# Attention, a mixture of four experts and a gated layer on one core: weight preparation issued earlier and in other steps

## Chip, core and metric

One core of one Trainium2 chip. The time is that of one execution on the device, in microseconds (us); the kernel before takes 738.04 us (median of three executions, 737.47 to 739.43). The engines run their own queues in order and meet at semaphores: TensorE (PE, with its weight loads as PEld), VectorE (DVE), ScalarE (ACT), GpSimd (POOL) and the queue that issues DMAs (SP).

## What is computed

Three layers in float32 precision, one feeding the next. `B, H, S, D = 2, 8, 576, 64`; 1152 tokens, model width 512.

```python
# 1. attention: heads 0..3 see the last 32 positions, heads 4..7 every 32nd one
scores = where(mask, q @ k.T / sqrt(64), -1e9)
attn = exp(scores - max); attn /= sum + 1e-9
x = (attn @ v) -> [1152, 512]
# 2. four experts, all applied to every token, mixed by normalised weights
p = domain_probs / (sum + 1e-9)
x = sum over e of p[:, e] * (relu(x @ w1[e]) @ w2[e])       # w1 512x1024, w2 1024x512
# 3. a gated layer; its three weights arrive as float64
out = (sigmoid(x @ w_gate) * (x @ w_val)) @ w_out            # 512x1536, 512x1536, 1536x512
```

## The kernel before

Every matrix product of layers 2 and 3 is done in halves: a float32 operand becomes a float16 part and a float16 remainder, and three products (high by high, high by low, low by high) are summed in PSUM (`split_products`, L552). Each operand is first scaled by a power of two found from its largest magnitude, on the chip.

**Units.** Layers 2 and 3 are 56 units. A unit is `("u", s, T)` (the first product of stage s on the T-th 288 tokens) or `("d", s, T)` (the second product). Stages 0 to 3 are the experts, 4 to 6 the three column blocks of the gated layer. A "u" unit of an expert has 8 PSUM tiles of 12 matmuls, a "d" unit of an expert 4 tiles of 24, so each has 96 matmuls of 288 columns. The order is u(0,0), d(0,0), u(0,1), d(0,1), ... for the first expert, and from then on u(1,0), u(1,1), d(1,0), u(1,2), d(1,1), ..., always with one "u" unit between a "u" and its "d".

**Attention** is a generator of 32 steps i = 0 to 31 (`attention`, L501). Step i normalises group i-1, multiplies group i-4 by the values, transposes the probabilities of group i-3, prepares queries and keys, and computes the scores of group i (24 groups). DVE takes the maximum, subtracts it and sums; ACT takes the exponential and copies PSUM tiles out. Steps 0 to 17 run in a loop of their own (`while 0 not in x_done`), because the first unit needs the scaled output of the first batch; steps 18 to 27 are issued inside u(0,0), one after every third group of three matmuls (`ATT_EVERY`); steps 28 to 31 stand between u(0,0) and d(0,0). `x_pair` scales a batch's result: it begins at step 15 for batch 0 and at step 27 for batch 1, with a maximum on DVE (L480, L485), a transpose on PE (L244) and a broadcast on PE (L250).

**Weights** come as 17 pieces (w1, w2 of each expert: pieces 0 to 7; gate, value and output block of each of three column blocks: 8 to 16). A piece is two raw tiles of 1 MB, which take turns in three buffers (`RAW_BUFS`). `prep_weights` is a generator, and each of its yields is one step:

- expert pieces: four maxima on DVE (L306), named R0 to R3 below; a last maximum over the four (L308), a transpose on PE (L244, "Ha") and a broadcast on PE (L250, "Hb"), after each of which the call ends ("hold"); then, once the weight buffer has room, four parts P0 to P3, each of them a scaled float16 copy on ACT (L332) and its remainder on DVE (L333, which reads what L332 wrote). Then it asks for two further raw tiles: their DMAs wait for the buffers that P1 and P3 release.
- float64 pieces: each half of a raw tile is turned into float32 by integer operations on DVE (`float32_of`, L263 to L279: L269, L271, L273, L275, L277, five steps), twice per raw tile; two maxima; Ha and Hb; then two parts with two ACT operations (L336, L337) and a remainder on POOL (L339).

Who calls it sets the order: `prep_some(n, steps)` goes on by so many steps. In the loop it is called with one step from i = 8 on, until piece 0 is done; in u(0,0) with one step after each of its 8 tiles; after the attention has ended, with two steps at each tile's "evac", which is before the instructions that empty that tile. Before a unit starts, what its own pieces still lack is prepared at once (L886).

**Emptying a tile.** In "u" units of experts ACT writes the float16 part and a copy (L595, L596), POOL the remainder (L597). In "d" units DVE scales the tile by the token weight into `t` (L616) and adds it to the sum over experts `x2acc` (L618); for the last expert it also takes the maximum (L620). After the last "d" tile of a T, `scale_x2` takes the maximum of four (L628), and `finish_x2`, a second generator that moves on once per tile (`go_late`), issues the transpose (L244), the broadcast (L250) and the scaled halves of the new x. Its first step is empty, so the transpose is issued one tile after L628.

The PE queue runs in order: a transpose Ha that waits for a DVE maximum holds all matmuls issued after it.

Of the kernel before, what the change touches and what calls it, by code (L numbers as in the profile page):

```python
# [9 lines left out]
F32 = mybir.dt.float32  # L10
# [8 lines left out]
PSUM = bass.MemoryType.PSUM  # L19

MASKED = -1.0e9
TOP = 2.0 ** 14
DOWN = 2.0 ** -24
W_BUFS = 2
# [12 lines left out]
def attn_moe_glu_kernel(ctx, tc, q, k, v, dp, w1, w2, wg, wv, wo, out):  # L37
# [48 lines left out]
    def load_local_qk(b, c):  # L86

        for nm, src in (("ql", q), ("kl", k)):
            t = atp.tile([TL, 2, 6 * D], F32, tag="raw" + nm, name="raw" + nm, bufs=1)
            nc.sync.dma_start(t, src[b, 2 * c:2 * c + 2].rearrange("h (p i) d -> p h (i d)", i=6))  # L90
            qkv["raw" + nm, b, c] = t
# [171 lines left out]
    def float32_of(f, r):  # L263

        words = r.bitcast(U32).rearrange("p (n z) -> p n z", z=2)
        lo_, hi_ = words[:, :, 0], words[:, :, 1]
        a = tmp["p"].tile([128, 512], U32, tag="bits", name="bits", bufs=1)
        m = tmp["p"].tile([128, 512], U32, tag="magn", name="magn", bufs=1)
        nc.vector.tensor_scalar(a, hi_, 5, 2, ALU.logical_shift_left, ALU.logical_shift_right)  # L269
        yield  # L270
        nc.vector.tensor_scalar(m, hi_, 1, None, ALU.logical_shift_left)  # L271
        yield
        nc.vector.scalar_tensor_tensor(a, hi_, 0xC0000000, a, ALU.bitwise_and, ALU.bitwise_or)  # L273
        yield
        nc.vector.scalar_tensor_tensor(a, lo_, 29, a, ALU.logical_shift_right, ALU.bitwise_or)  # L275
        yield
        nc.vector.scalar_tensor_tensor(  # L277
            f, m, float(897 << 21), a.bitcast(F32), ALU.is_ge, ALU.mult)
        yield  # L279

    peak_n = [0]
# [318 lines left out]
    def g2(e, T):  # L600
        pc = 2 * e + 1
        hh, hl = H.pop((e, T))
        col = e * NT + T
        cc = comb[:, col:col + 1]
        nc.vector.tensor_scalar(cc, down[:, 2 * e:2 * e + 1], down[:, SX + T:SX + T + 1], 1.0 / DOWN, ALU.mult, ALU.mult)
        nc.vector.tensor_tensor(cc, cc, down[:, pc:pc + 1], ALU.mult)
        for kk in range(KC):
            ps = g_tile()[:, :TC]
            yield from split_products(ps, [
                (wh[pc][:, fb, kk * 128:(kk + 1) * 128], wl[pc][:, fb, kk * 128:(kk + 1) * 128],  # L610
                 hh[fb], hl[fb]) for fb in range(FB)
            ])
            yield "evac"
            a = acc["x2"][:, kk, T * TC:(T + 1) * TC]
            t = a if e == 0 else scratch()
            nc.vector.scalar_tensor_tensor(t, ps, cc, pb[e, T], ALU.mult, ALU.mult)  # L616
            if e:
                nc.vector.tensor_tensor(a, a, t, ALU.add)  # L618
            if e == E - 1:
                nc.vector.tensor_reduce(  # L620
                    peak[:, 8 + kk:9 + kk], a, AX.X, ALU.max, apply_absolute_value=True)
            yield "tile"
        if e == E - 1:
            yield from scale_x2(T)
# [8 lines left out]

    def finish_x2(T, scale):

        yield
        yield from scale
        yield
        col = SX2 + T
        alloc_x(T)  # L640
        for kk in range(KC):
            a = acc["x2"][:, kk, T * TC:(T + 1) * TC]
            dh, dl = xh[T][:, kk, :], xl[T][:, kk, :]
            nc.scalar.activation(dh, a, AF.Copy, scale=up[:, col:col + 1])
            nc.vector.scalar_tensor_tensor(dl, a, up[:, col:col + 1], dh, ALU.mult, ALU.subtract)
        for r in range(T * TC // 128, -(-(T + 1) * TC // 128)):
            n = min((T + 1) * TC - r * 128, 128)
            if n == 128 and r * 128 >= T * TC:
                nc.vector.tensor_scalar(row_down[:, r:r + 1], down[:, col:col + 1], 1.0 / DOWN, None, ALU.mult)
            elif n < 128:  # L650
                nc.vector.tensor_scalar(row_down[:n, r:r + 1], down[:n, col:col + 1], 1.0 / DOWN, None, ALU.mult)
            else:
                p0 = T * TC - r * 128
                for q0, q1 in ((32, 64), (64, 96), (96, 128)):
                    if q0 >= p0:
                        nc.vector.tensor_scalar(
                            row_down[q0:q1, r:r + 1], down[q0:q1, col:col + 1], 1.0 / DOWN, None, ALU.mult)
        yield
# [154 lines left out]
    with tc.manual_schedule():  # L813
        load_strided_qk(0, 0)
        load_strided_qk(0, 1)
        load_strided_v(0, 0)
        load_local_qk(0, 0)
        load_strided_v(0, 1)
        load_local_v(0, 0)
        warm_up()  # L820
        make_constants()
        nc.scalar.activation(top[:, 0:1], ones[:, 0:1], AF.Exp)
        for T in range(NT):
            alloc_x(T)

        def more_loads():

            yield load_raw_to(1)
            yield load_local_qk(0, 1)
            yield load_local_v(0, 1)  # L830
            yield load_raw_to(2)
            yield load_strided_qk(1, 0)
            yield load_strided_v(1, 0)
            yield load_strided_qk(1, 1)
            yield nc.sync.dma_start(ptok, dp.rearrange("(t p) e -> p t e", p=128))
            yield load_local_qk(1, 0)
            yield load_strided_v(1, 1)
            yield load_local_v(1, 0)
            yield load_local_qk(1, 1)
            yield load_local_v(1, 1)  # L840
            yield load_raw_to(RAW_BUFS)


        load_at = {0: 1, 2: 1, 3: 2, 4: 1, 5: 1, 6: 1, 7: 1, 8: 1, 10: 1, 12: 1, 14: 1, 15: 1, 16: 1}
        mix_at = {1: (0, 0), 5: (0, 1), 13: (1, 0), 17: (1, 1)}
        loads = more_loads()

        def attend():
            i = next(att, None)
            if i is None:  # L850
                return None
            for _ in range(load_at.get(i, 0)):
                next(loads, None)
            if i in mix_at:
                mix_heads(*mix_at[i])
            if i == 12:
                token_weights()
            if i == 14:
                spread_token_weights()
            return i  # L860

        def end_attention():
            at_stack.close()
            accp = ctx.enter_context(tc.tile_pool(name="accp", bufs=1, side="right", reuse_waits="tile"))
            tmp["acc"] = accp
            tmp["p"] = ctx.enter_context(tc.tile_pool(name="tmp", bufs=2, side="right", reuse_waits="tile"))
            tmp["h"] = ctx.enter_context(tc.tile_pool(name="hp2", bufs=1, side="right", reuse_waits="tile"))
            tmp["g"] = ctx.enter_context(
                tc.tile_pool(name="gp2", bufs=8 - PSUM_BUFS, space=PSUM, side="right", reuse_waits="tile"))
            tmp["w"] = ctx.enter_context(tc.tile_pool(name="wp2", bufs=W_BUFS_2, side="right", reuse_waits="tile"))  # L870
            acc["x2"] = accp.tile([128, KC, NTOK], F32, tag="acc", name="x2acc")

        att = attention()
        while 0 not in x_done:
            i = attend()
            keep_warm(WARM_STEP)

            if i >= 8 and (going or todo[0] == 0):
                prep_some(0, 1)
        n_none = 0  # L880
        for n, u in enumerate(units):
            if n == 1:
                while "p" not in tmp:
                    if attend() is None:
                        end_attention()
            while any(i in pieces_of(u) for i in waiting()):  # L886
                prep_some(n, 1)
            if u[0] == "u" and u[1] >= E:
                go_late(u[2])
            if u == ("d", E, 0):  # L890
                go_late(NT - 1)
                acc["out"] = tmp["acc"].tile([128, NTB, DM], F32, tag="acc", name="outacc")
            load_p_some(n)
            load_p_some(n)
            for y in unit_steps(u):
                if "p" not in tmp and y is None:
                    n_none += 1
                    if n_none % ATT_EVERY == 0 and attend() is None:
                        end_attention()
                if y == ("tile" if "p" not in tmp else "evac"):  # L900
                    prep_some(n, 2 if "p" in tmp else 1)
                if y == "tile":
                    go_late()

# [27 lines left out]
```

## Time and profile before

The profiled execution took 736.88 us, of which 735.0 us lie between its first and last instruction; the median of the runs is 738.04 us.

| engine | busy us | share of the span | instructions |
|---|---|---|---|
| PE | 689.6 | 94% | 5702 |
| DVE | 419.9 | 57% | 812 |
| ACT | 265.8 | 36% | 568 |
| POOL | 210.0 | 29% | 257 |

The first unit's first matmul starts at 74.3 us, the unit d(0,0) at 115.3, u(0,1) at 136.5, u(4,0) at 501.8; the last instruction ends at 735.0. Unit borders are found by counting the matmuls of `split_products` in the order of time: 96 for each unit of an expert.

"Busy" is the time covered by instructions; a duration is that of one instruction; the idle time in brackets in a timeline is what the engine stood still before that instruction, and after the arrow is what ended it. The granted TensorE clock has two levels here, 1.2 and 2.4 GHz, and a stretch's mean of 0.70 means that it ran at half speed for 60% of it.

### The profile page before, as it was taken

Reading aid. Unit: us, or ns where it says so; the run is one execution under the profiler, and the core shown is the slowest. Engines: PE = TensorE matmul, PEld = TensorE weight load, DVE = VectorE, ACT = ScalarE, POOL = GpSimd, SP = SyncE. Lnnn points to the kernel's source line nnn. Section 1 sums busy time; section 2 is a strip of 40 time slices with the busy share of each in tenths; the row PEclk is TensorE's granted clock in tenths of the full one; section 3 lists DMA queues with packets and bytes.
Section 4 is the critical chain, followed back from the end, with each engine's and each line's share of the span. In section 5 each row is a group of like instructions: output and inputs, shape, how many; then the busy total and the mean of one; then the engine's idle time right before and its main releaser. Section 6 shows DMA issues by size and latency. Waiting matters only on the chain.

```text
span 735.0 us, 13594 instructions
## 1 busy us (share of the span) xinstructions
PE 689.6 (94%) x5702; PEld 512.6 (70%) x5713; DVE 419.9 (57%) x812; ACT 265.8 (36%) x568; POOL 210.0 (29%) x257
## 2 busy tenths in 40 slices
PE   8888695989998999999999999988899999999998
PEld 5656473767776777777777777767676666676774
DVE  2585867671066212639317797878887696822122
ACT  3544554433245125232324244252235344231220
POOL 4221230313214123114324272440224244141110
PEclk8997996989999999999999999999999999999999
DMA  8914302330033000304200221111111310000001
GB/s 220 229 30 123 131 2 91 138 133 9 9 123 115 7 4 10 123 9 172 66 9 26 99 66 58 58 58 58 58 58 58 115 58 1 1 1 1 29 29 72
DMA packets 26765, 48.88 MB, mean 67 GB/s; under 512 B 9324, under 2 KB 13200, under 8 KB 26704
## 3 DMA queue, kind: packets, MB, share of 16 engines
q1 hardware_dynamic: 26704, 48.02, 20.7%
q8 instruction: 45, 0.74, 0.4%
q14 instruction: 16, 0.13, 0.1%
HBM read 45.63 MB, written 2.38 MB: 65 GB/s over the span
## 4 chain that ended last, share of the span: by engine, by line
PE 74%; DVE 15%; ACT 5%; issue 2%; DMA 2%; POOL 1%; SPq 0%; ACTq 0%; DVEq 0%
PE gps L556 22%; PE gps L558 22%; PE gps L557 22%; DVE pk L306 3%; PE sps L412 2%; DVE wl L333 2%; ACT wh L332 1%; DVE cv L277 1%; DVE x2acc L618 1%; DVE t L616 1%; DMA ks<-in_k_dram 1%; DMA raw<-in_moe_w_dram 1%; DVE bits L275 1%; PE o L464 1%; DVE bits L273 1%
## 5 line engine op out<-in xcount | busy, mean ns | idle before, releaser
L557 PE MATMUL gps<-xl,wh 128*128 128x288 f16 x896 | 257.8, 288 | 1.1 <-DVE xl L495 1.1
L556 PE MATMUL gps<-xh,wh 128*128 128x288 f16 x896 | 258.0, 288 | 0.3 <-ACT xh L494 0.3
L558 PE MATMUL gps<-xh,wl 128*128 128x288 f16 x896 | 257.7, 288 | 0.0
L597 POOL TENSOR_TENSOR hl<-t,hh 128x288 f16<-128x288 f32 x128 | 104.8, 825 | 259.6 <-ACT t L596 256.3
L556 PEld LDWEIGHTS <-wh 128*128 128x128 f16 x1408 | 138.5, 98 | 41.4 <-ACT wh L332 4.5
L558 PEld LDWEIGHTS <-wl 128*128 128x128 f16 x1408 | 138.7, 99 | 39.5 <-DVE wl L333 2.3
L557 PEld LDWEIGHTS <-wh 128*128 128x128 f16 x1408 | 138.7, 98 | 36.2 <-issue 0.6
L556 PE MATMUL gps<-hh,wh 128*128 128x288 f16 x512 | 148.0, 289 | 3.7 <-ACT wh L332 3.7
L558 PE MATMUL gps<-hh,wl 128*128 128x288 f16 x512 | 147.9, 289 | 1.3 <-DVE wl L333 0.7
L557 PE MATMUL gps<-hl,wh 128*128 128x288 f16 x512 | 148.0, 289 | 0.0
L595 ACT ACTIVATE hh<-gps 128x288 f16<-128x288 f32 x128 | 52.4, 410 | 197.3 <-PE gps L558 197.3
L694 POOL TENSOR_TENSOR hl<-t,hh 128x288 f16<-128x288 f32 x48 | 37.5, 782 | 145.4 <-ACT hh L693 145.4
L616 DVE SCALAR_TENSOR_TENSOR t<-gps,comb,pb 128x288 f32<-128x288 f32 x48 | 24.6, 513 | 83.5 <-PE gps L558 82.1
L333 DVE SCALAR_TENSOR_TENSOR wl<-raw,up,wh 128x1024 f16<-128x1024 f32 x32 | 40.4, 1299 | 39.4 <-ACT wh L332 39.4
L596 ACT ACTIVATE t<-gps 128x288 f32<-128x288 f32 x128 | 51.9, 406 | 9.2 <-POOL hl L597 9.0
L692 DVE SCALAR_TENSOR_TENSOR t<-gps,sg 128x288 f32<-128x288 f32 x48 | 21.8, 454 | 54.0 <-PE gps L558 41.7
L339 POOL TENSOR_TENSOR wl<-cv,wh 128x1024 f16<-128x1024 f32 x18 | 40.3, 2239 | 40.5 <-ACT wh L337 40.5
L693 ACT CAST hh<-t 128x288 f16<-128x288 f32 x48 | 20.7, 431 | 80.8 <-DVE t L692 80.8
L332 ACT ACTIVATE wh<-raw,up 128x1024 f16<-128x1024 f32 x32 | 34.9, 1141 | 24.3 <-DVE up L236 13.4
L556 PE MATMUL gps<-wh,hh 128*128 128x512 f16 (+1 forms) x112 | 41.6, 371 | 0.0
L557 PE MATMUL gps<-wl,hh 128*128 128x512 f16 (+1 forms) x112 | 41.6, 371 | 0.0
L558 PE MATMUL gps<-wh,hl 128*128 128x512 f16 (+1 forms) x112 | 41.6, 371 | 0.0
(121 smaller groups left out, 727.0 us busy)
## 6 DMA issues: line engine op xcount, KB each, us to landing
raw<-in_moe_w_dram SPq DMA_DIRECT2D x16, 1024.0 KB
raw<-in_moe_w_gate_dram SPq DMA_DIRECT2D x6, 1024.0 KB
raw<-in_moe_w_val_dram SPq DMA_DIRECT2D x6, 1024.0 KB
raw<-in_moe_w_out_dram SPq DMA_DIRECT2D x6, 1024.0 KB
pb<-pd SPq DMA_DIRECT2D x15, 144.0 KB
out_dram<-outacc SPq DMA_DIRECT2D x8, 256.0 KB
vl<-in_v_dram SPq DMA_DIRECT2D x8, 192.0 KB
qs<-in_q_dram SPq DMA_DIRECT2D x4, 288.0 KB
```

The source lines that it names most:

```text
L306: nc.vector.tensor_reduce(pk[:, n:n + 1], part, AX.XY, ALU.max, apply_absolute_value=True)
L332: nc.scalar.activation(hi_, part, AF.Copy, scale=up[:, i:i + 1])
L333: nc.vector.scalar_tensor_tensor(lo_, part, up[:, i:i + 1], hi_, ALU.mult, ALU.subtract)
L339: nc.gpsimd.tensor_tensor(lo_, part, hi_, ALU.subtract)
L556: nc.tensor.matmul(ps, ah, bh, start=i == 0, stop=False)
L557: nc.tensor.matmul(ps, ah, bl, start=False, stop=False)
L558: nc.tensor.matmul(ps, al, bh, start=False, stop=i == n - 1)
L595: nc.scalar.activation(hh[fb], ps, AF.Relu, scale=DOWN)
L596: nc.scalar.activation(t, ps, AF.Relu, scale=DOWN)
L597: nc.gpsimd.tensor_tensor(hl[fb], t, hh[fb], ALU.subtract)
L616: nc.vector.scalar_tensor_tensor(t, ps, cc, pb[e, T], ALU.mult, ALU.mult)
L694: nc.gpsimd.tensor_tensor(dl, gv, dh, ALU.subtract)
```

## The change

In words: (1) in the attention loop `prep_some` is called from i = 6, with two steps at i = 6 and 7, and goes on to piece 1 from i = 16; inside u(0,0) it is also called with one step after every attention step, and with two steps instead of one after every tile. (2) The second raw tile is asked for before the values of heads 2 and 3, the third at i = 6 instead of i = 16, which puts it in front of four loads of batch 1. (3) In `float32_of` the magnitude is taken by ACT (`Abs`) in the first step, so there are four steps instead of five; the threshold is compared as a float. (4) The addition to `x2acc` goes from DVE to POOL. (5) `finish_x2` has one more empty step in front.

```diff
+LEAST = 2.0 ** -15 * 1.125
...
-        m = tmp["p"].tile([128, 512], U32, tag="magn", name="magn", bufs=1)
+        m = tmp["p"].tile([128, 512], F32, tag="magn", name="magn", bufs=1)
         nc.vector.tensor_scalar(a, hi_, 5, 2, ALU.logical_shift_left, ALU.logical_shift_right)
-        yield
-        nc.vector.tensor_scalar(m, hi_, 1, None, ALU.logical_shift_left)
+
+        nc.scalar.activation(m, hi_.bitcast(F32), AF.Abs)
         yield
...
         nc.vector.scalar_tensor_tensor(
-            f, m, float(897 << 21), a.bitcast(F32), ALU.is_ge, ALU.mult)
+            f, m, LEAST, a.bitcast(F32), ALU.is_ge, ALU.mult)
...
             if e:
-                nc.vector.tensor_tensor(a, a, t, ALU.add)
+                nc.gpsimd.tensor_tensor(a, a, t, ALU.add)
...
     def finish_x2(T, scale):
 
+        yield
         yield
         yield from scale
...
             yield load_raw_to(1)
             yield load_local_qk(0, 1)
+            yield load_raw_to(2)
             yield load_local_v(0, 1)
-            yield load_raw_to(2)
             yield load_strided_qk(1, 0)
             yield load_strided_v(1, 0)
+            yield load_raw_to(RAW_BUFS)
             yield load_strided_qk(1, 1)
...
-            yield load_raw_to(RAW_BUFS)
...
-        load_at = {0: 1, 2: 1, 3: 2, 4: 1, 5: 1, 6: 1, 7: 1, 8: 1, 10: 1, 12: 1, 14: 1, 15: 1, 16: 1}
+        load_at = {0: 1, 2: 2, 3: 1, 4: 1, 5: 1, 6: 1, 7: 1, 8: 2, 10: 1, 12: 1, 14: 1, 15: 1}
...
-            if i >= 8 and (going or todo[0] == 0):
-                prep_some(0, 1)
+            if 6 <= i and (going or todo[0] == 0 or i >= 16):
+                prep_some(0, 2 if i == 6 or i == 7 else 1)
...
-                    if n_none % ATT_EVERY == 0 and attend() is None:
-                        end_attention()
+                    if n_none % ATT_EVERY == 0:
+                        if attend() is None:
+                            end_attention()
+                        else:
+                            prep_some(n, 1)
                 if y == ("tile" if "p" not in tmp else "evac"):
-                    prep_some(n, 2 if "p" in tmp else 1)
+                    prep_some(n)
```

## Rows read from the trace of the kernel before

**Rows 1.** The page: busy us and share; the granted clock in 40 slices.

```profile
PE 689.6 (94%) x5702; PEld 512.6 (70%) x5713; DVE 419.9 (57%) x812; ACT 265.8 (36%) x568; POOL 210.0 (29%) x257
...
PEclk8997996989999999999999999999999999999999
```

**Rows 2.** The waits of PE: us in total, times, longest.

```profile
PE gps L244 <- DVE pk L308: 10.7, 5, 4.2
...
PE gps L244 <- DVE peak L628: 6.3, 4, 2.1
PE peaks L244 <- DVE peak L485: 4.0, 2, 2.8
PE gps L556 <- ACT wh L332: 3.7, 1, 3.7
```

**Rows 3.** Stretches: length, busy of PE, PEld, DVE, ACT, POOL, clock, DMA, GB/s.

```profile
45.90:60.25 14.35, 12.50 (x179) 8.97 (x179) 11.91 (x37) 7.19 (x21) 5.05 (x11) 1.00 0.16 45
...
92.07:103.60 11.53, 11.53 (x156) 8.33 (x153) 9.65 (x25) 5.81 (x18) 4.82 (x7) 1.00 0.01 3
...
115.30:136.50 21.20, 16.22 (x101) 10.56 (x100) 14.21 (x26) 6.90 (x12) 0.73 (x1) 0.70 0.33 114
136.50:155.70 19.20, 14.98 (x100) 10.79 (x100) 12.02 (x17) 10.68 (x20) 6.51 (x7) 0.82 0.30 110
...
203.30:215.00 11.70, 11.70 (x98) 9.36 (x96) 9.74 (x11) 4.86 (x6) 0.96 (x2) 1.00 0.51 179
215.00:227.30 12.30, 12.30 (x101) 9.70 (x100) 7.62 (x12) 8.48 (x17) 4.91 (x5) 1.00 0.23 65
227.30:242.60 15.30, 12.51 (x102) 9.65 (x100) 5.93 (x11) 6.08 (x17) 7.26 (x11) 1.00 0.27 97
301.40:314.40 13.00, 12.38 (x100) 9.59 (x99) 5.07 (x12) 5.09 (x14) 4.85 (x7) 1.00 0.06 21
...
471.20:487.90 16.70, 13.16 (x104) 9.83 (x103) 14.29 (x34) 6.75 (x19) 5.33 (x7) 1.00 0.34 123
487.90:501.80 13.90, 12.03 (x99) 9.42 (x99) 10.42 (x21) 4.74 (x6) 5.18 (x3) 1.00 0.00 1
```

**Rows 4.** Timelines of ACT and PE around attention step 18.

```profile
78.14 2.17 ACT L332 ACTIVATE wh<-raw,up 128x1024 f16<-128x1024 f32 x2
...
82.95 0.27 PE L377 MATMUL qkps<-ident,ql 96*128 96x96 f32 x1 [4.01 <-ACT PT L443]
```

**Rows 5.** Timeline of PE between the first two units.

```profile
113.56 0.27 PE L244 MATMUL peaks<-ident,peak 128*1 128x128 f32 x1 [2.78 <-DVE peak L485]
...
122.83 0.42 PE L556 MATMUL gps<-hh,wh 128*128 128x288 f16 x1 [3.71 <-ACT wh L332]
```

**Rows 6.** The chain that ended last, 136 to 160 us.

```profile
140.68 6.41 DMA raw<-in_moe_w_dram
```

**Rows 7.** Groups by line and form: busy us, mean ns, idle before.

```profile
L333 DVE SCALAR_TENSOR_TENSOR wl<-raw,up,wh 128x1024 f16<-128x1024 f32 x32 | 40.4, 1299 | 39.4 <-ACT wh L332 39.4
...
L306 DVE TENSOR_REDUCE pk<-raw 128x1 f32<-128x1024 f32 x32 | 37.7, 1208 | 1.3 <-DMA raw<-in_moe_w_dram 1.3
L332 ACT ACTIVATE wh<-raw,up 128x1024 f16<-128x1024 f32 x32 | 34.9, 1141 | 24.3 <-DVE up L236 13.4 <-PE gps L557 10.9
...
L618 DVE TENSOR_TENSOR x2acc<-x2acc,t 128x288 f32<-128x288 f32 x48 | 25.7, 535 | 1.6
...
L271 DVE TENSOR_SCALAR magn<-raw 128x512 uint32<-128x512 uint32 x36 | 19.4, 539 | 0.0
...
L428 POOL TENSOR_TENSOR P<-P,sm 128x288 f32<-128x288 f32 x24 | 16.0, 667 | 63.9 <-DVE sm L427 49.6 <-ACT ksT L384 4.7 <-PE o L474 3.1
```

**Rows 8.** Timelines of POOL and DVE in d(3,2).

```profile
490.65 4.45 POOL L339 TENSOR_TENSOR wl<-cv,wh 128x1024 f16<-128x1024 f32 x2 [1.48 <-ACT wh L337]
...
491.61 1.49 DVE L618 TENSOR_TENSOR x2acc<-x2acc,t 128x288 f32<-128x288 f32 x1
...
501.36 0.16 DVE L628 TENSOR_REDUCE peak<-peak 128x1 f32<-128x4 f32 x1
```

## The prediction

> **What bounds the kernel now.** First the page's busy times: PE is busy for 689.6 of 735.0 us [rows 1], so at most 45 us are idle, and every gain must come from PE's idle time or from its slow clock. Next the waits of PE [rows 2]: no engine's throughput stops it, but single late results do. Two kinds concern a transpose Ha that waits for a maximum of DVE: a weight piece's (10.7 us in 5) and the x2 scale's (6.3 in 4). Attention has 4.0 for batch maxima, d(0,0) 3.7 for a weight part. Then the table of stretches [rows 3] shows where: a unit of 96 matmuls at full clock takes 11.7 us (203.30:215.00, PE busy throughout), 0.12 each, so an expert "u" tile is 1.47 us and a "d" tile 2.94. Against that d(0,0) takes 21.2 at a mean clock of 0.70, u(0,1) 19.2 at 0.82, u(1,1) 15.3, u(3,3) 16.7, d(3,2) 13.9. The clock costs (1 - 0.70) x 21.2 = 6.4 and (1 - 0.82) x 19.2 = 3.5 us there, part of it on top of the idle time. Last the timelines: they name the late result at each place [rows 4, 5, 6].
>
> The sum is made against the profiled execution, 736.88 us; the median of the runs is 738.04, 1.16 above it. I add that back at the end.
>
> **Where each step lands.** Counting the calls by the code: before, R0 to R3 of piece 0 stand at i = 8 to 11 and P0 to P3 at i = 15, 16, 17 and in front of u(0,0); piece 1 gets one step per tile of u(0,0), so that its P2 and P3 come after the attention. After: R0 to R3 at i = 6, 7, the holds at 8 to 10, P0 to P3 at 11 to 14, R0 to R2 of piece 1 at 15 to 17. In u(0,0) there are 10 + 8 x 2 steps for 8: R3 at i = 18, Ha and Hb by the second tile, P0 at i = 20, P1 at i = 21, P2 and P3 behind the third tile, R0 of piece 2 at i = 22, R1 and R2 behind the fourth tile, R3 at i = 23. After its Ha and Hb, by i = 25, piece 2 only waits for room, which it has from d(0,0) on.
>
> **Part 1, the attention loop.** A part costs DVE 1.30 us and a wait for ACT's 1.14 us half; that wait averages 39.4 / 32 = 1.23 us [rows 7]. DVE's own attention work is about 1.95 us per step: 9.65 busy in four steps (92.07:103.60) less one and a half maxima of 1.21 [rows 3, 7]. With a part a step takes DVE 1.95 + 1.30 + 1.23 = 4.5 us; PE takes 14.35 / 4 = 3.6 per step at i = 11 to 14 [rows 3]. DVE falls behind by 0.9 x 4 = 3.6 us; what shows is between 0 (three score tiles lie ahead) and 3.6, as PE waits at i = 15 for a batch maximum behind all this; I take +2.5. Two maxima a step at i = 6 and 7 make DVE 1.95 + 2.42 = 4.4 us against 3.6: +0.5, between 0 and 1.6. The three maxima at 15 to 17 hide behind PE. Against that, two ACT halves leave step 18 [rows 4]: PE waits 4.01 us there behind 2.17 us of them, so -2.2; and P1's half no longer precedes the first x at i = 17, -1.1 (bounds 0 and its 1.14). The sum is -0.3, from -3.3 to +3.
>
> The third raw tile, 1 MB, goes before four batch 1 loads on SP. A lone raw tile takes 6.4 us [rows 6], the DMA queues are nearly empty from 45 to 60 us (share 0.16 [rows 3]), and these loads are used from step 12 on. I cost it at 0; if the cover fails, 6.4 at most.
>
> **Part 2, u(0,0) and d(0,0).** At i = 20 to 23 DVE gets 4 x 1.95 + 4 x 1.30 + three waits of 1.23 + 4 x 1.21 = 21.5 us in a stretch where PE needs 11.5 and idles nowhere [rows 3, 7]. It falls behind by 10 us. Two steps of 2.9 us fit in the score tiles; so +4, between 0 and 10. Steps 24 to 27 have no weight work, and DVE catches up there. So the maximum for x_pair at i = 27 no longer stands behind P0's remainder (1.30 us [rows 7]): of PE's 2.78 us wait for it [rows 5] I take half off, -1.4, between 0 and all of it. From that transpose to the end of d(0,0) it is 136.5 - 113.56 = 22.9 us now; work is left there for 6 + 96 matmuls x 0.1225 and a broadcast, 12.8. Piece 1 is ready, so the 3.71 us wait for a weight part [rows 5] goes, and with the idle time, I take it, the slow clock. Half a us is kept for the last remainder of POOL: -9.6, between -5 (slow clock stays) and -10. Part 2: 4.0 - 1.4 - 9.6 = -7.0.
>
> **Part 3, pieces 3 and 4.** Ha of a piece comes a fixed number of tiles behind P0 of the one before it, and between them lie P0, P1, a 6.41 us raw DMA that waits for P1's buffer, and two maxima [rows 6]. Piece 3 has five "u" tiles, 7.35 us, for this now and PE idles 4.2 us (longest in [rows 2]). After, P0 stands behind the first tile of d(0,0) and Ha behind the second of u(0,1): 3 x 2.94 + 2 x 1.47 = 11.8 us, as for piece 5, whose Ha in 215.00:227.30 costs nothing (12.30 busy of 12.30) [rows 3]. So u(0,1) falls from 19.2 to 12.3, like that unit: -6.9. Piece 4 then has 4 x 1.47 + 2.94 = 8.8 us. Piece 6, with 7.35, idles 2.8 (227.30:242.60) [rows 3]; less the 1.47 more that gives 1.3, and against piece 3's 4.2 it gives 2.7. I take +1.5. Part 3: -5.4, from -7 to -3.5. From unit 7 on the steps of expert pieces fall where they did.
>
> **Part 4, fourth expert on.** Idle now: of the 10.7 us of piece maxima [rows 2], 4.2 lie in u(0,1), 2.8 in u(1,1) and 0.6 in u(2,0) [rows 3], so 3.1 are left; with 6.3 for the four scales, 9.4 us. What changes:
> - `Abs` takes away 36 DVE instructions of 0.54 us [rows 7], 19 us in all, and 36 steps. A unit still makes two steps per tile, so a conversion ends earlier, but DVE's load per tile does not fall. On ACT it has no row; the 1024 column L332 takes 1.14 [rows 7], so at most that and above 0; half, 0.6, is taken. ACT is idle for over half of u(3,3) (6.75 busy of 16.70 [rows 3]), which hides it: 0; uncovered, 36 x 0.6 = 21 us of ACT.
> - The addition frees 0.535 us on DVE 48 times; for the second and third expert nothing waited for it, so 0. For the fourth, the maximum L620 behind it must now wait for POOL, and the next tile's steps behind L620. POOL's two-input L428 takes 0.67 [rows 7]; L339, 2.23 for 1024 columns [rows 8], gives 0.63 for 288. With both hand-overs I take 0.9, between 0.63 and the 1.49 of an addition that was slow on DVE [rows 8]. So each tile is 0.4 later and the maximum of a T 1.5: just the 1.47 that the x2 transpose now waits longer. Where POOL has two L339 in the same unit (d(3,2), 490.65 to 495.10 [rows 8]) the additions stand behind them, and I take 2.0.
> - Earlier conversions move the maxima: piece 10's out of u(3,2) into d(3,0), piece 11's into d(3,1), so DVE has less in front of the first two scales. Scales: d(3,2)'s 1.9 (13.90 less 12.03 [rows 3]) becomes 1.9 + 2.0 - 1.5 = 2.4; d(3,3)'s, the longest, goes from 2.1 to 1.6, as its L339 come late in the unit; the first two, 2.3 together, to 0.5. So 6.3 becomes 4.5. Pieces: 3.1 becomes 2.0, of which 1.2 is new (piece 12's Ha, now behind the first tile of d(3,3)). Together -2.9, between -8 and +3.
>
> The Trainium skill, "GPSIMD Engine Reference", section "Engine selection", puts GpSimd at about twice VectorE's time for elementwise operations of two inputs. By it an addition would take 1.07, some 0.4 more than L428 shows, the three scale waits that are left would grow by 1.6 each, and the sum would come out 4.8 later, a weaker form of rival 1. The trace does not bear it out: 0.67 against 0.535.
>
> **Sum.** -0.3 - 7.0 - 5.4 - 2.9 = -15.6: 736.88 - 15.6 = 721.3, and with 1.16 added 722.4 us.
>
> **Rivals.**
> 1. *POOL becomes DVE's brake.* In the fourth expert's "d" units DVE stops for POOL in all 16 tiles; if additions cost 1.49 each, a T's maximum is 4 x 0.95 = 3.8 us later, 2.3 more than the delay buys: four scales + 9.3, less some 6 that the moved maxima free in front of the first two, less 1.1 for the pieces. Part 4 is then +2.2, the time 727.5. For: [rows 8] show the addition on DVE at 1.49 against its mean of 0.535 while POOL runs. Against: POOL has 29% load [rows 1]. Chance 0.20.
> 2. *The new DVE load in attention takes the gain back.* One mechanism: DVE stands behind ACT's weight halves at i = 11 to 14 and 20 to 23, its delay exceeds the three score tiles, PE idles, and its clock halves as it does around d(0,0). Price: part 1 then +3.6 + 0.5 - 1.1 and, at d(0,0)'s clock of 0.70, 0.3 x 14.35 = 4.3, so +7.3; part 2 +10 + 6.4 - 11 = +5.4. With parts 3 and 4: +4.4, time 742.4, slower. It decides from a delay of some 6 us on. For: 21.5 us of DVE work in 11.5. Against: a step without weight work frees DVE for 1 to 1.6 us. Chance 0.07; half of it (only u(0,0), no slow clock) gives 722.4 + 6 = 728.4: 0.13.
> 3. *Attention gets its full clock throughout*, as its idle spots go: the slice from 55 to 74 us now has 0.7 [rows 1], 0.3 x 18.4 = 5.5; and part 2's +4 does not show. Time 722.4 - 9.5 = 713. Against: the loop's waits only change place. Chance 0.10.
>
> The forecast has 0.50, with its own range of 717 to 727. The range 712 to 733 takes in rivals 1 and 3 and the weak form of 2. This kernel's measurement tells 0.3%, 2.2 us, from no change. Faster: 0.50 + 0.20 + 0.13 + 0.10 less 0.04 of tails, 0.89; same 0.04; slower 0.07.
>
> **What would show it.** Right: no PE wait for a weight part in d(0,0), which takes about 12 us at full clock; u(0,1) near 12.3 and d(0,1) near 13.5; PE waits for L620's T maxima of 1 to 2.5 us, and DVE idling before L620 for POOL. Wrong: DVE waits of PE above 6 us in u(0,0); a clock below 1 after 90 us; first matmul of u(0,0) more than 4 us from 74.3; idle between 440 and 560 us above 10.

## Result: slower, and where the profile after has the time

The changed kernel takes 745.62 us (median; 741.29 to 748.0 in eight executions) against 737.46 for the kernel before on the same chip (eight executions): ratio 1.0099, 95% interval 1.0069 to 1.0128. The forecast was 722.4, its range 712 to 733. The profiled execution took 746.48 us, span 744.7. Line numbers after are one higher than before up to L636 (L306 is L307, L332 is L333).

Busy times on the page, answering to [rows 1]: DVE has lost 41 us, POOL has gained 42, ACT 21, as the change says. PE has 10 us more for the same matmuls: from 20 us on its clock was at its lower level for 51.2 us in the kernel after and for 34.1 in the kernel before.

```profile
PE 700.1 (94%) x5713; PEld 518.4 (70%) x5713; DVE 379.0 (51%) x728; ACT 286.5 (38%) x604; POOL 251.9 (34%) x305
...
PEclk8976697999999999999999999899999999999999
```

The waits of PE, answering to [rows 2] (total, times, longest). A weight piece's maximum has grown from 10.7 us in 5 to 16.7 in 8, and 2.6 more at a "peaks" transpose; the wait for a weight part in d(0,0) is gone, and of the x2 scale's 6.3 there is 4.0 left (2.3 of them listed under the tiny instruction behind the maximum, `comb`).

```profile
PE gps L245 <- DVE pk L309: 16.7, 8, 4.5
...
PE peaks L245 <- DVE pk L309: 2.6, 1, 2.6
PE gps L245 <- DVE comb L680: 2.3, 1, 2.3
```

Stretches of the kernel after, answering to [rows 3]: length, busy PE, PEld, DVE, ACT, POOL, clock, DMA share, GB/s. They are a part of the attention loop, u(0,0), d(0,0), u(0,1), d(0,1), u(3,3).

```profile
42.49:66.38 23.89, 22.43 (x197) 14.99 (x197) 12.73 (x34) 10.96 (x24) 4.38 (x8) 0.57 0.06 17
84.40:131.60 47.20, 37.16 (x398) 26.07 (x396) 31.36 (x71) 22.37 (x55) 12.55 (x18) 0.86 0.15 52
131.60:143.40 11.80, 11.80 (x98) 9.44 (x98) 10.89 (x20) 8.23 (x14) 0.73 (x1) 1.00 0.24 88
143.40:157.30 13.90, 12.49 (x102) 9.62 (x101) 10.74 (x16) 8.48 (x17) 4.93 (x5) 1.00 0.37 124
157.30:171.00 13.70, 12.38 (x101) 9.57 (x99) 6.69 (x14) 1.10 (x3) 2.31 (x4) 1.00 0.29 109
471.65:491.47 19.82, 15.27 (x104) 10.93 (x102) 9.55 (x30) 6.61 (x18) 7.11 (x10) 0.83 0.15 53
```

Taken from the first matmul of each unit in both traces (the -2.2 us of attention step 18, which the prediction counts in its part 1, stand in the row of u(0,0), where that step is issued):

| place | predicted | measured |
|---|---|---|
| attention loop (first unit from 74.3 to 84.4) | +1.9 | +10.1 |
| u(0,0) | +0.4 | +6.3 |
| d(0,0) | -9.6 | -9.5 |
| u(0,1) | -6.9 | -5.4 |
| d(0,1) | +1.5 | +2.0 |
| from there to 435 us | 0 | -1.3 |
| from 435 us to the end | -2.9 | +7.4 |
| sum (span) | -15.6 | +9.7 |

The loop's 10.1 us are nearly all clock: from 20 us to the first unit PE's idle time is 7.7 us for 7.3, and the clock is at its lower level for 30.7 us in place of 10.2. Of the 6.3 in u(0,0), 1.9 are idle time of PE (10.04 us against 8.17); the other 4.4 are busy time, with the clock at its lower level for 13.7 us in place of 4.5.

The loop at 35 to 41 us in the kernel after (start, us, engine, line, operation; in brackets the idle time before it and what ended it):

```profile
35.65 2.33 DVE L307 TENSOR_REDUCE pk<-raw 128x1 f32<-128x1024 f32 x2
...
39.14 0.46 DVE L420 TENSOR_TENSOR P<-sps,nm 128x288 f32<-128x288 f32 x1
...
39.69 0.44 ACT L421 ACTIVATE P<-P 128x288 f32<-128x288 f32 x1 [3.14 <-DVE pk L309]
...
40.49 0.52 ACT L448 COPY PT<-tps 96x384 f32<-96x384 f32 x1
...
41.06 0.47 PE L371 MATMUL qkps<-ident,ks 72*128 72x72 f32 x4 [2.27 <-ACT PT L448]
```

Two maxima stand in front of a score tile's subtraction, so its exponential is late; the copy that frees a PSUM tile is behind that exponential on ACT; PE waits for the tile 2.27 us. From 42.49 us on the granted clock is 0.57 over 23.89 us, at its lower level (1.2 GHz) for 20.5 of them. Before, it was at its upper level from 45.90 to 60.25 us [rows 3].

### The profile page after: what moved, and what is told of

It is laid out like the page before. It is cut to its first block, busy times and chain, and to the rows that moved or that the text cites. A ratio compares the mean times of both kernels' runs of the same rounds, so it can differ in the third digit from the quotient of the medians.

```text
span 744.7 us, 13646 instructions
## 1 busy us (share of the span) xinstructions
PE 700.1 (94%) x5713; PEld 518.4 (70%) x5713; DVE 379.0 (51%) x728; ACT 286.5 (38%) x604; POOL 251.9 (34%) x305
## 4 chain that ended last, share of the span: by engine, by line
PE 69%; DVE 18%; ACT 6%; issue 3%; POOL 2%; DMA 1%; SPq 0%; DVEq 0%; ACTq 0%; POOLq 0%
PE gps L557 21%; PE gps L558 21%; PE gps L559 21%; DVE pk L307 4%; DVE wl L334 2%; PE sps L413 2%; ACT wh L333 2%; DVE bits L276 2%; DVE bits L274 2%; POOL wl L340 1%; DVE P L420 1%; DVE bits L270 1%; DVE nm L419 1%; POOL x2acc L619 1%; DMA ks<-in_k_dram 1%
## 5 line engine op out<-in xcount | busy, mean ns | idle before, releaser
L598 POOL TENSOR_TENSOR hl<-t,hh 128x288 f16<-128x288 f32 x128 | 107.2, 844 | 159.1 <-ACT t L597 159.0
L557 PE MATMUL gps<-hh,wh 128*128 128x288 f16 x512 | 146.5, 286 | 0.0
L559 PE MATMUL gps<-hh,wl 128*128 128x288 f16 x512 | 146.4, 286 | 0.0
L558 PE MATMUL gps<-hl,wh 128*128 128x288 f16 x512 | 146.4, 286 | 0.0
L696 POOL TENSOR_TENSOR hl<-t,hh 128x288 f16<-128x288 f32 x48 | 38.0, 792 | 143.1 <-ACT hh L695 142.4
L619 POOL TENSOR_TENSOR x2acc<-x2acc,t 128x288 f32<-128x288 f32 x48 | 40.3, 841 | 76.6 <-DVE t L617 72.8
L429 POOL TENSOR_TENSOR P<-P,sm 128x288 f32<-128x288 f32 x24 | 16.0, 666 | 77.5 <-DVE sm L428 62.8
```

The costliest lines, as they stand in the source:

```text
L557: nc.tensor.matmul(ps, ah, bh, start=i == 0, stop=False)
L558: nc.tensor.matmul(ps, ah, bl, start=False, stop=False)
L559: nc.tensor.matmul(ps, al, bh, start=False, stop=i == n - 1)
L598: nc.gpsimd.tensor_tensor(hl[fb], t, hh[fb], ALU.subtract)
L619: nc.gpsimd.tensor_tensor(a, a, t, ALU.add)
L696: nc.gpsimd.tensor_tensor(dl, gv, dh, ALU.subtract)
```

## Experiments

All are compared with the kernel before on the same chip (its median 737.1 to 737.9). The four parts of the change come first, each alone on the kernel before.

**The attention part alone** (call pattern and order of the raw loads; the loads' lines are those of the change and are left out here).

```
...
-            if i >= 8 and (going or todo[0] == 0):
-                prep_some(0, 1)
+            if 6 <= i and (going or todo[0] == 0 or i >= 16):
+                prep_some(0, 2 if i == 6 or i == 7 else 1)
...
+                        else:
+                            prep_some(n, 1)
...
-                    prep_some(n, 2 if "p" in tmp else 1)
+                    prep_some(n)
```

> The kernel before with parts 1 and 2 of the change alone (call pattern of the preparation, order of the raw loads). Theory: the attention loop loses about 10 us to the doubled maxima at i = 6 and 7 and to the parts at 11 to 14, through idle PE and half clock; u(0,0) loses about 6; d(0,0) gives back 9.5, u(0,1) and d(0,1) together 3 to 4. So 739 to 741, 2 to 3 us above before, and piece maxima after 440 us as before (3 us of PE wait). Rival, that the parts help each other and the late stages suffer from the shift: 743 or more, with PE waits after 440 us above 12.

739.39 us, ratio 1.0022 (0.9992 to 1.0051), not told apart from the kernel before. First unit at 85.2, u(0,0) 46.0 us, d(0,0) 11.8, idle spot of 2.27 us at 38.84: the first 171 us are those of the kernel after, and the 9.5 us that d(0,0) gains are given back ahead of it.

**The sums on POOL alone.**

```
-                nc.vector.tensor_tensor(a, a, t, ALU.add)
+                nc.gpsimd.tensor_tensor(a, a, t, ALU.add)
```

> The kernel before with the addition on POOL alone. Theory: the maximum behind it (L620) waits 0.9 us or more for POOL 16 times, DVE loses 0.45 us net per tile of the fourth expert, and each x2 scale wait grows by 1 to 2: 741 to 744. Rival, that DVE has slack in these units and only the last tile's lateness counts: scale waits grow by 0.5 each, 738 to 740. Rival, that freeing DVE pays: 735 or less.

743.29 us, ratio 1.0089 (1.0058 to 1.012). Waits of PE, and of DVE, from 435 to 560 us:

```profile
PE gps L244 <- DVE peak L628: 10.9, 4, 3.1
```

```profile
DVE peak L620 <- POOL x2acc L618: 16.6, 16, 2.0
```

Each of the 16 maxima waits for POOL, and the four scale waits grow from 6.3 to 10.9 us.

**The magnitude on ScalarE alone** (one step of five goes with it).

```
...
-        yield
-        nc.vector.tensor_scalar(m, hi_, 1, None, ALU.logical_shift_left)
+        nc.scalar.activation(m, hi_.bitcast(F32), AF.Abs)
...
```

> The kernel before with Abs on ScalarE and four steps alone. Theory: conversions end a fifth earlier in the order of issue while DVE is no faster per tile, so the transposes of the piece maxima stand earlier in PE's queue than DVE can serve them: piece maxima wait 8 to 11 us after 330 us instead of 3 to 4, time 742 to 745. Rival, that the freed 19 us of DVE pay: 733 to 736.

745.07 us, ratio 1.0103 (1.0073 to 1.0134).

**The x2 scale a tile later alone.**

```
     def finish_x2(T, scale):
         yield
+        yield
```

> The kernel before with the x2 scale one tile later alone. Theory: the four scale waits of 0.7, 1.6, 1.9 and 2.1 us shrink by one tile of 1.47 each, to 0, 0.1, 0.4, 0.7: 5 us less, 732 to 733. Rival, that DVE simply stands behind and the wait moves to the next piece maximum: 736 to 738.

731.27 us, ratio 0.992 (0.9893 to 0.9947): faster. The four parts give +1.5, +5.4, +7.2 and -6.6 us, together +7.5, against +8.2 for the whole. Each is known to about 2 us either way; within that they add up, so each is looked at by itself.

**Why the magnitude costs.** Two kernels, each a change to the magnitude on ScalarE alone: two buffers (`bufs=2` for `magn`), and one buffer with an empty step (`yield`) in the place of the one taken out.

> The magnitude on ScalarE alone, with two buffers for it in place of one (745.1 us with one; 36 Abs, before which ACT waits 35.1 us for the L278 product that reads the buffer). Theory 1: ACT stands still for that product, the relus and conversions queued behind the Abs come late, and with them the maxima; with two buffers ACT's wait falls below 10 us, PE's waits for pk go from 13.4 back to 8 or so, and the time is 738 to 740. Theory 2: what makes the pieces late is that one step in five is gone, so that Ha is issued earlier than DVE can have the maximum ready; then ACT's wait goes, PE's waits for pk stay at 12 to 14, and the time stays at 743 to 746.

> The magnitude on ScalarE alone, one buffer, but the fifth step kept as an empty one, so that every later step and every Ha is issued at the same tile as in the kernel before. Theory 2 (the missing step is the cause): no PE wait for pk beyond those of before (10.7 us in 5), the x2 scale waits smaller than 6.3 since DVE has 36 instructions of 0.54 us less, time 735 to 738. Theory 1 (ACT's wait for the one buffer is the cause): PE's waits for pk stay above 12 and the time at 742 to 746.

Two buffers: 746.38 us, ratio 1.0112 (1.0073 to 1.0152). Step kept: 737.41, ratio 0.9998 (0.9969 to 1.0026). What ACT waits for with one buffer and the step left out:

```profile
ACT magn L272 <- DVE cv L278: 35.1, 16, 6.5
```

What ACT waits for, and what PE waits for from 460 us on, in the kernel with two buffers (before, PE waits there for pk 3.1 us in 2 and for the scales 5.6 in 3):

```profile
ACT magn L272 <- DVE cv L278: 4.5, 3, 2.0
```

```profile
PE gps L245 <- DVE pk L309: 7.0, 5, 2.8
PE gps L245 <- DVE peak L629: 5.9, 3, 2.3
```

And in the kernel with the step kept:

```profile
ACT magn L272 <- DVE cv L279: 45.5, 17, 9.9
```

```profile
PE gps L245 <- DVE peak L630: 4.0, 2, 2.1
PE gps L245 <- DVE pk L310: 1.9, 1, 1.9
```

The two cross: without ACT's wait (35.1 us with one buffer, 4.5 here) the time stays bad, and with a longer one (45.5) it is that of before. So it is not ACT. The missing step issues every later step, and with them Ha, earlier on PE's queue, while DVE still has the maximum to do. In u(3,3) of the kernel after, PE and DVE at that place:

```profile
473.51 2.34 DVE L307 TENSOR_REDUCE pk<-cv 128x1 f32<-128x1024 f32 x2
...
477.54 0.14 DVE L309 TENSOR_REDUCE pk<-pk 128x1 f32<-128x2 f32 x1
```

```profile
477.83 0.37 PE L245 MATMUL gps<-ident,pk 128*1 128x128 f32 x1 [4.55 <-DVE pk L309]
```

Ha was next for PE at 473.28, and DVE had not begun the two maxima.

**Which of the sums cost**: the second and third expert's on POOL, the fourth's on DVE.

```
-                nc.vector.tensor_tensor(a, a, t, ALU.add)
+                (nc.vector if e == E - 1 else nc.gpsimd).tensor_tensor(a, a, t, ALU.add)
```

> The expert sums on POOL for the second and third expert alone (32 of 48); the fourth expert's, whose maximum follows on DVE, stay on DVE. With all on POOL it was 743.3 us, x2 scale waits 10.9 in 4 against 6.3. Theory: only the sums that a DVE maximum waits for cost; then the scale waits are back at 6.3 and the time at 736 to 739. Rival: POOL's additions hold up other things of POOL or of a port it shares with DVE, in all experts; then 740 or more, with DVE's instructions beside them longer than in the kernel before.

736.77 us, ratio 0.9991 (0.997 to 1.0012); scale waits 5.6 in 3. 32 of 48 additions on POOL cost and bring nothing that the interval shows; the 16 that a maximum waits for are the 5.4 us.

**The doubled maxima at i = 6, 7.** The attention part alone with one step there, and, in another kernel, with ten matmuls on zeros put into PE's idle spot.

```
-                prep_some(0, 2 if i == 6 or i == 7 else 1)
+                prep_some(0, 1)
```

> The attention part alone, with one weight step a call at i = 6 and 7 where it has two (so the four maxima of piece 0 stand at i = 6 to 9, its parts at 13 to 16). Theory: the doubled maxima in front of a score tile's subtraction on DVE delay an exponential, PE idles 2.27 us at 38.84 in the attention part alone, and the clock is 0.5 from 42.3 to 66.2 behind that. Then here no idle of PE above 1 us between 35 and 45 us, full clock from 42 to about 60, the first expert unit at 76 to 79 us in place of 85.2, and a time 6 to 9 us under the attention part alone (739.4), 730 to 733. Rival: it is the added load of DVE at i = 11 to 14 and in u(0,0); then the half clock comes anyway from about 50 us on, the first unit starts at 82 or later, and the time stays at 737 to 740.

```
+                if (kind, nm, half, b, c) == ("s", "k", 0, 1, 0):
+                    keep_warm(10)
```

> The attention part alone, with ten more matmuls of 512 columns on zeros (their result is read by nothing) put on PE just where it stood idle for 2.27 us at 38.84. DVE's and ACT's work is unchanged, and so is the late exponential; only PE's idle time is filled. Theory: it is that idle spot that the clock falls behind; then the granted clock stays at 1 from 42 to about 60, the first expert unit starts at 76 to 80 in place of 85.2, though PE has 2 us more work, and the time is 732 to 737. Rival: the clock falls because the loop as a whole has gaps behind DVE; then the stretch of 24 us at 0.5 stays, only a little moved, the unit starts at 84 to 87 and the time is 739 to 742.

The stretch from 42.2 to 55 us in the attention part alone, with single steps, and with the spot filled (columns as above; the clock is the third number from the end):

```profile
42.20:55.00 12.80, 11.99 (x92) 8.12 (x91) 4.96 (x16) 4.68 (x11) 1.33 (x2) 0.50 0.17 34
```

```profile
42.20:55.00 12.80, 11.54 (x166) 8.17 (x168) 8.94 (x31) 6.09 (x18) 4.12 (x8) 1.00 0.21 39
```

```profile
42.20:55.00 12.80, 10.28 (x148) 7.40 (x147) 8.59 (x26) 6.75 (x16) 2.18 (x5) 1.00 0.25 55
```

At the lower clock PE is as busy and does 92 matmuls for the 166 of single steps. With single steps the first unit starts at 77.5 in place of 85.2; with the spot filled, the doubled maxima still there and 2.35 us more work on PE, at 78.9. In these profiled executions it is the idle spot that the clock falls behind. Four kernels have the doubled maxima and an empty spot: the kernel after, the attention part alone, and the two of the next paragraph that are built on the kernel after. Each has the hole of 2.27 us, with the lower clock at most 1.5 us behind it, and a first unit at 84.1 to 85.2 us; the eleven kernels with the loop of before have it at 72.1 to 75.1. The times follow less: 739.48 us with single steps (0.9982 to 1.0038), where 730 to 733 were expected, and 738.23 with the spot filled (0.9984 to 1.0049), where 732 to 737 were. With single steps u(0,0) takes 53.0 us in place of 46.0, and what the loop gains is lost there: PE waits 5.52 us for piece 2's maximum in place of 2.45, and the clock is at its lower level for 27.3 us in place of 10.2. With the spot filled, the profiled execution does keep the loop's gain, but its 734.18 us are near the lowest of ten (733.45 to 743.5). So what the hole costs the loop is shown in the profiled executions; that the median gets it back is not.

**u(0,0).** Of the attention part only the further steps in u(0,0) and the raw loads, with the loop of before:

> Of the attention part only the further steps at the calls in u(0,0) and the order of the raw loads; the loop ahead of the expert units has one step a call from i = 8, as before. Theory: the loop's start then comes back to 74 to 76 us, d(0,0) keeps its 11.8 us, and u(0,0) pays for DVE's added work as in the attention part alone, 46 to 50 us in place of 41; the end of d(0,0) is at 132 to 136 (before 136.5), the end of d(0,1) within 2 us of before's 167.5, and the time 735 to 739: nothing gained. Rival: u(0,0) was long only since the loop ahead of it ran late; then it takes 41 to 43, d(0,0) ends at 128 to 130 and the time is 729 to 732.

735.97 us, ratio 0.9981 (0.9954 to 1.0007), d(0,0) 11.8, end of d(0,1) at 167.6: as the theory said, though u(0,0) took 54.7, more than its 46 to 50. The trace of it names what is late:

```profile
107.17 1.28 DVE L333 SCALAR_TENSOR_TENSOR wl<-raw,up,wh 128x1024 f16<-128x1024 f32 x1 [1.55 <-ACT wh L332]
...
108.38 2.34 DVE L306 TENSOR_REDUCE pk<-raw 128x1 f32<-128x1024 f32 x2
...
112.24 2.33 DVE L306 TENSOR_REDUCE pk<-raw 128x1 f32<-128x1024 f32 x2
...
114.61 0.16 DVE L308 TENSOR_REDUCE pk<-pk 128x1 f32<-128x4 f32 x1
...
114.91 0.37 PE L244 MATMUL peaks<-ident,pk 128*1 128x128 f32 x1 [5.51 <-DVE pk L308]
```

These are the maxima and the Ha of piece 2, behind piece 1's last part. No unit uses piece 2 before the ninth. Two kernels give the further steps to piece 1 alone: one with the loop of before and the x2 scale a tile later, one on the kernel after with the step kept and the fourth expert's sums on DVE. That last base was also run by itself:

> The kernel after with two things taken back: the fifth step of a conversion is kept as an empty one, and the fourth expert's sums stay on DVE. If these two are the whole loss behind 430 us, only the attention part (+1.5) and the gain of the x2 scale (-6.6) are left: 732 to 734, no idle of PE above 2 us behind 440, and the first 170 us as in the kernel after. If the parts work on each other otherwise, 738 or more.

735.29 us, ratio 0.9968 (0.9943 to 0.9994), no idle spot above 1.4 us behind 440: the two parts taken back are the loss there, though the time is 1.3 us above what was expected.

```
-                        else:
+                        elif going and going[0][1] < 2:
                             prep_some(n, 1)
```

> The further steps in u(0,0) without the changed loop ahead of it, but given to piece 1 alone (piece 2, which no unit needs before the ninth, gets no step more than before there), with the x2 scale a tile later. Theory: what costs in u(0,0) is not piece 1's work but that of piece 2: its four maxima stand on DVE in front of score tiles' work, and its transpose Ha is issued where DVE has them 5.51 us late. Then no wait for pk above 1 us is left in u(0,0), u(0,0) takes 41 to 46 us in place of 54.7, d(0,0) keeps 11.8, the end of d(0,1) is at 160 to 165 (before 167.5), and the time 722 to 728. Rival: piece 1's own parts and maxima are the load; then u(0,0) takes 47 us or more, the end of d(0,1) is at 166 to 168, and the time is that of the x2 scale alone, 730 to 733.

> The kernel after with the fifth step kept, the fourth expert's sums on DVE (735.3 us so), and the further steps in u(0,0) for piece 1 alone. Theory: the 2.4 us wait for piece 2's maximum and some slow clock go from u(0,0), which takes 40 to 44 us in place of 46.0; the doubled maxima's 2.27 us idle spot and the half clock behind it stay: 729 to 733. Rival: nothing of it comes from piece 2; then 734 to 737.

729.08 us, ratio 0.9885 (0.9866 to 0.9904), u(0,0) 50.0; and 733.26, ratio 0.9942 (0.9923 to 0.9962), u(0,0) 45.8. Both times lie between theory and rival; the first one's u(0,0) is the rival's (47 or more). The first has no wait for pk in u(0,0) any more, but piece 2's four maxima still come in with the ordinary two steps per tile, and PE waits 3.53 us behind them for an attention tile (L474). The last run keeps piece 2 out of u(0,0):

```
-                if i >= 2 * E and "p" not in tmp:
+                if i >= 2 * E and "p" not in tmp or i >= 2 and n == 0:
                     return
```

> As p1_x2 (729.1 us), but piece 2 does not begin before d(0,0): in p1_x2 its four maxima of 1.17 us still came into u(0,0) with the ordinary two steps per tile, at 109 to 115 us, and PE waited 3.53 us behind them for an attention tile. Theory: these maxima, put between the softmax steps of a DVE that is already late, make u(0,0) long; without them the waits of 3.53 and 1.49 us go, u(0,0) takes 42 to 46 us in place of 50.0, d(0,1) ends at 156 to 160 in place of 163.4, and the time is 723 to 726. Rival: the four parts of piece 1, on DVE at 100 to 109 us, make it; then u(0,0) takes 48 or more and the time is 728 to 731.

724.68 us, ratio 0.9849 (0.9804 to 0.9894; two of its six executions took 730.2 and 731.6): faster than both kernels. Its u(0,0), d(0,0), u(0,1) and d(0,1):

```profile
73.30:119.00 45.70, 34.91 (x395) 25.01 (x395) 31.81 (x70) 24.94 (x57) 13.00 (x18) 0.89 0.31 106
119.00:130.90 11.90, 11.90 (x99) 9.51 (x99) 10.08 (x21) 3.98 (x10) 0.73 (x1) 1.00 0.01 1
130.90:148.20 17.30, 14.31 (x103) 10.36 (x100) 11.51 (x16) 9.06 (x19) 6.51 (x7) 0.90 0.34 123
148.20:160.00 11.80, 11.80 (x98) 9.43 (x98) 11.28 (x15) 4.77 (x6) 0.73 (x1) 1.00 0.50 177
```

The further steps for piece 1 cost u(0,0) 4.7 us; piece 2's maxima were 4.4 more in the run before it (50.0 to 45.6), with the same loop and the same x2 step.

**A later Ha for every piece from the third on**, on the kernel with the x2 scale a tile later:

```
         yield "hold"
+        if i >= 2:
+            yield "hold"
         for _ in scale_on_chip(i, pk[:, 4:5], 6 + i % 2):
```

> The x2 scale a tile later alone, and for every piece from the third on one more empty step between its last maximum and its transpose Ha. If Ha waits for its maximum only because it is issued a fixed number of tiles behind it, and a step in between settles that, the waits of 4.2, 2.8, 1.9 and 1.1 us for pk go (some 10 us together), with the half clock of 6.8 us at 148.3 behind the first; nothing is late for it, since the pieces are ready several units ahead. Time 731.3 - 10 to - 12: 719 to 722. Rival: DVE is short of time there, and the wait moves to the parts or to the next piece; then 728 to 732.

732.99 us, ratio 0.993 (0.9903 to 0.9956), not told apart from the 731.27 without it. Against that kernel the wait for pk in u(1,1) is 1.4 us in place of 2.8, and two of 1.1 behind 470 us are gone, but the one in u(0,1) is 3.5 in place of 2.9, and a scale now waits:

```profile
520.42 2.34 DVE L306 TENSOR_REDUCE pk<-cv 128x1 f32<-128x1024 f32 x2
...
524.19 0.16 DVE L630 TENSOR_REDUCE peak<-peak 128x1 f32<-128x4 f32 x1
```

```profile
524.41 0.27 PE L244 MATMUL gps<-ident,peak 128*1 128x128 f32 x1 [4.14 <-DVE peak L630]
```

The 719 to 722 of the theory did not come. The rival held in kind, 1 us above its 728 to 732: the wait moves, here to a scale, whose maximum stands behind a piece's two.

## Why the prediction was wrong, step by step

Of the 25.3 us between the forecast span and the measured one, 8.2 lie in the attention loop, 5.9 in u(0,0) and 10.3 behind 435 us.

**Part 1 failed at the doubled maxima.** The step was "+0.5, between 0 and 1.6", from DVE's 4.4 us against PE's 3.6 per step. It compared sums over a step; what counted was the order in it. Two maxima in one piece, 2.33 us, stood in front of one subtraction, and through ACT's queue that made a 2.27 us hole in PE, above the 1.6, behind which the clock was at its lower level. The clock was the larger miss: some 7 us in the profiled executions (84.1 to 85.2 against 77.5 with single steps). Rival 2 had this chain, DVE late, PE idle, clock halved, but at i = 11 to 14 and 20 to 23. The gain at step 18 (-2.2) came, inside u(0,0): its 4.01 us wait is a 1.94 one.

**Part 2's d(0,0) was right**, -9.5 against -9.6, with the full clock and no wait, and the x_pair wait fell from 2.78 to 1.40, by the 1.4 forecast. **Its u(0,0) failed by its "+4, between 0 and 10"**, which measured 9.7 (6.28, plus the 1.38 and the 2.07 that went from the two waits in that unit). The prediction counted piece 2's four maxima there, as part of 21.5 us of DVE work, and its Ha by i = 25, but put no wait on that Ha (2.57 us in the kernel after) and no clock on any of it (4.4 us), nor did it ask whether a unit soon needs that piece. With piece 1 alone the term is 6.1 (4.7 plus 1.4).

**Part 3** was right in kind: u(0,1) 13.9 at full clock (forecast 12.3), d(0,1) 13.8 (13.3). Together -3.4 for -5.4, just short of its range of -7 to -3.5.

**Part 4 failed at "Earlier conversions move the maxima"**, which made piece waits fall from 3.1 to 2.0. They are 11.2 from 435 us on, and behind the longest, 4.55, the clock is at its lower level for 6.8 us more:

```profile
PE gps L245 <- DVE pk L309: 11.2, 5, 4.5
```

The prediction saw that a conversion ends earlier with a step less, and that DVE's load per tile does not fall; it should have drawn the consequence that it drew for piece 3: Ha comes a fixed number of tiles after the start, so a step less moves Ha toward PE while the maximum stays where DVE can do it. The scales were right (4.0 for 4.5), and so was `Abs` at 0 on ACT (the two kernels that cross).

**The addition was mis-sized.** DVE stands idle before the 16 maxima of the kernel after:

```profile
DVE peak L621 <- POOL x2acc L619: 19.1, 16, 2.3
```

That is 1.19 per tile against the 0.535 that went, +0.66 where the prediction had +0.4 and rival 1 +0.95. Alone it makes the scales 4.6 us later (6.3 to 10.9), which is rival 1's mechanism; in the kernel after, the extra tile for x2 hides most of it, as forecast (4.0 us of scale waits). The addition took 0.84 on POOL, 1.57 times the 0.535 of DVE [rows 7]. The Trainium skill, "GPSIMD Engine Reference", section "Engine selection", says about twice for elementwise operations of two inputs. The prediction chose the row of a multiplication (L428, 0.67) over it; the measured 0.84 lies between the two.

Of the signs named in advance, three of the four against came: the first matmul of u(0,0) 10 us late, a clock below 1 after 90 us (which the kernel before has too, around d(0,0)), and idle above 10 us between 440 and 560 (11.9, before 9.5). PE's waits for DVE in u(0,0) stayed below 6. Of the signs for it, d(0,0) without a wait, the scale waits of 1 to 2.5 us and DVE's idle time before L620 came as well: they belong to the steps that were right.

## What to carry to other kernels

Where steps are issued by count, a step is also a delay: taking an instruction out of a chain pulls every later issue forward, and an in-order engine then meets a wait for a result that is no sooner ready; keep the step as an empty one and look at what is next in each queue. Before work is brought forward into a tight stretch, ask of every piece of it whether a unit soon needs it: here bringing forward piece 1 gained and piece 2 lost it again. Price a new hole in PE with the clock that may follow it, and not with its length alone. Where single executions of one kernel differ by several us, read a mechanism from the profile and its worth from the medians.

## What the runs showed of the hardware

After a hole of 2.27 us in PE the granted clock stood at its lower level for 23.9 us on end in the attention part alone (42.29 to 66.18), with PE busy for 11.99 of 12.80 us in the stretch shown; ten matmuls on zeros in the hole, 2.35 us, and it stayed at the upper level there. In the sums on POOL alone, stretches of 3.41 us at the lower level stand at three of the four scale waits (2.32, 2.98 and 2.51 us; from 448.41, 506.44 and 533.75 us on), 1.7 us each beside the wait, and none at the longest, 3.11 us. One and the same wait, 2.79 us for pk in u(1,1), has such a stretch behind it in seven profiled executions, those of the POOL, magnitude and x2 parts alone among them, and none in eight, those of the kernel before, the kernel after and the attention part alone among them. So the length of a wait alone does not tell what the clock does; what else decides is not shown. Executions of one kernel differ by several us: 734.8 to 742.3 in 24 of the kernel before on one chip, 733.8 to 743.2 in ten of the attention part alone. Why the clock's path in the first 130 us differs from one execution to the next stays open.
